# A fused attention and MLP kernel, re-planned: a longer transfer list for GpSimd, turned tiles stored by one transfer, a shorter weight decode, and three more chunks with halved own-key scores

## The chip, the cores and the metric

The kernel runs on one core of a Trainium2 chip. The metric is the device time of one execution in microseconds (us), less being better. The engines are called PE (TensorE, the matrix engine), DVE (VectorE), ACT (ScalarE), POOL (GpSimd) and SP (SyncE, which here only starts transfers). TensorE's weight loads (PEld) are listed apart from its matmuls (PE).

## The reference

Two sequences of S = 3136 tokens pass through three stages: an attention without softmax, a gated MLP with a convolution of three taps along the tokens, and a normalised MLP with a residual.

```python
scores = matmul(z, z.transpose(0, 2, 1)) / S          # z: 2 x 3136 x 64
x   = u * matmul(maximum(scores, 0) ** 2, v)          # u, v: 2 x 3136 x 256
h   = maximum(x @ w_in, 0)                            # 256 -> 1024
c   = conv of h over tokens, 3 taps per feature (conv_w), zero padded
x   = (h / (1 + exp(-c))) @ w_out                     # 1024 -> 256
xn  = (x - mean) / sqrt(var + 1e-6) * g_ln            # over the 256 features
out = x + maximum(xn @ w_ch1, 0) @ w_ch2
```

The weights arrive as float64.

## The kernel before

**Stages.** The 3136 queries of each sequence are cut into seven chunks of 4, 4, 3, 4, 3, 3 and 3.5 tiles of 128 (`TILES`), so there are 14 chunks, c = 0 to 13. For a chunk, each of the 25 key tiles j gives a score tile (two matmuls, `products`), which ACT passes through ReLU and squares, and which is split into a high part `ah` (a rounding cast) and a low part `al` (a subtraction on DVE), because each product is made of three matmuls, high by high, low by high and high by low (`av`). When all 25 keys are summed in the PSUM tile `av`, DVE multiplies by u (`gate_u`, op `gate_x`) and the result goes to DRAM. The MLPs run over 17 blocks of 384 or 256 tokens (`make_x`, `mlps`), interleaved with later chunks; the last two blocks, 256 tokens each, are the tail and share PSUM tiles.

**Scores used twice.** Scores are symmetric. A score tile of chunk c whose keys lie in a later chunk of the same sequence is turned 32 by 32 by DVE (`spill`, tile `bl`), stored to DRAM (`turned`), and loaded instead of computed when that later chunk comes (`land`, four transfers per tile, one for each group of 32 partitions, each by SP or POOL as the planner chooses). For four pairs of chunks (`EARLY`) the blocks are instead exchanged at the store: four transfers write `mirror`, and one transfer loads a tile. For the chunks in `HALVED`, the scores of a chunk's queries with its own keys are computed on one side of the diagonal alone (`corner` columns less); the other side is turned and stored (`spill_corner`) and loaded by four transfers per tile (`land_corner`).

**Weights.** Each of the 16 pieces of 512 weights per partition (and the small `conv_w`) is turned from float64 words into a high and a low float part by `decode`: ACT takes the absolute value, DVE makes several passes with integer operations, ACT or POOL casts and converts.

**Order.** A planner in the kernel's Python (`Program`) fixes the order of all instructions on each engine before anything runs. Every operation has a price (`PRICE`), a time after which others see its result (`AFTER`, `late`), and a due time that is worked back from its users; `once` plays the program through with these prices, always taking the ready operation that is due first, and `order` keeps the best of ten rounds. A block of the MLPs gets its due time from the end of its chunk plus a lag (`LAG0`, falling with c). POOL and SP take their instructions strictly in that order, transfers included. Where the plan leaves TensorE a gap, `fill` puts matmuls on a tile of zeros into it, one for each 0.125 us of planned gap (`FILL`), and twenty of them (`WARM`) stand ahead of everything.

[...]

## Time and profile before

| what | us |
|---|---|
| median of three runs | 1085.47 |
| lowest and highest | 1083.96 and 1085.91 |
| profiled execution, its own time | 1084.57 |
| span in the profile, first to last instruction | 1082.6 |

The profile gives busy time by engine, the span cut into 40 slices, the chain of work that ended last, groups of instructions by line, and who waited for whom. [...]

### The profile page before, as it was taken

The page shows a single profiled execution, that of the slowest core. Times are in us where ns is not written, and L with a number is a line of the kernel's source. Part 1 is how long each engine was busy: PE and PEld are TensorE (multiplying, and loading weights), DVE is VectorE, ACT ScalarE, POOL GpSimd, SP SyncE. Part 2 cuts the span into 40 slices and gives each one's busy share as a digit, 9 for nine tenths or more (in the row PEclk, how much of TensorE's full clock was granted, in tenths as well). Part 3 has the DMA queues.
Part 4 walks back from the last instruction along what each step waited for, and adds up shares of the span by engine and source line. Part 5 has one row for each costly group of instructions (what it writes and reads, how often), then busy time and mean ns, then how long its engine had stood idle before and what let it go on. Part 6 is the DMA issues. An engine that isn't in the chain of part 4 may idle for free.

```text
span 1082.6 us, 19738 instructions
## 1 busy us (share of the span) xinstructions
PE 1069.0 (99%) x6508; PEld 1008.7 (93%) x6508; DVE 873.6 (81%) x1888; ACT 732.6 (68%) x1530; POOL 170.7 (16%) x266
## 2 busy tenths in 40 slices
PE   9999999999999999999999999999999999999998
PEld 7777997999999999999999999999999999999998
DVE  7999998999887877787868879678778594878674
ACT  7788987777677766676757667566566474656553
POOL 2011112323131000000010101111222324310000
PEclk9999999999999999999999999999999999999999
DMA  6787867677677331324253424342644646430000
GB/s 205 203 210 159 211 164 172 163 179 194 177 177 180 97 112 49 102 80 124 55 134 103 120 52 122 93 110 66 151 89 109 139 94 153 97 85 26 18 23 21
DMA packets 312166, 130.42 MB, mean 120 GB/s; under 512 B 203920, under 2 KB 298528, under 8 KB 312064
## 3 DMA queue, kind: packets, MB, share of 16 engines
q1 hardware_dynamic: 304928, 117.49, 43.2%
q0 software_dynamic: 7136, 11.67, 4.9%
q8 instruction: 51, 0.84, 0.3%
q14 instruction: 51, 0.42, 0.1%
HBM read 72.21 MB, written 53.94 MB: 117 GB/s over the span
## 4 chain that ended last, share of the span: by engine, by line
PE 90%; DVE 3%; DMA 2%; issue 2%; ACT 2%; POOL 0%; SPq 0%; DVEq 0%; ACTq 0%
PE av L908 12%; PE av L911 12%; PE av L910 11%; PE y L1015 8%; PE y L1017 8%; PE y L1016 8%; PE h2ps L999 4%; PE hps L999 4%; PE h2ps L1000 4%; PE h2ps L1001 4%; PE hps L1001 4%; PE hps L1000 4%; PE s L866 3%; PE s L867 3%; DMA land<-turned 1%
## 5 line engine op out<-in xcount | busy, mean ns | idle before, releaser
L908 PE MATMUL av<-ah,vh 128*128 128x512 f32 (+2 forms) x700 | 257.0, 367 | 2.5 <-DVE u L926 2.1
L911 PE MATMUL av<-ah,vl 128*128 128x512 f32 (+2 forms) x700 | 256.0, 366 | 0.0
L910 PE MATMUL av<-al,vh 128*128 128x384 f32 (+2 forms) x672 | 246.7, 367 | 3.9 <-DVE al L842 3.9
L804 POOL DMA_DIRECT2D land<-turned x202 | 129.7, 643 | 449.4 <-DVE al L842 171.4
L908 PEld LDWEIGHTS av<-ah,vh 128*128 128x128 f32 x700 | 131.6, 188 | 14.6 <-DVE u L926 2.3
L911 PEld LDWEIGHTS av<-ah,vl 128*128 128x128 f32 x700 | 131.5, 188 | 14.3
L910 PEld LDWEIGHTS av<-al,vh 128*128 128x128 f32 x672 | 126.3, 188 | 16.1 <-DVE al L842 6.2
L1259 ACT ACTIVATE g2h<-h2ps 128x384 fp32r<-128x384 f32 (+1 forms) x136 | 65.2, 480 | 111.4 <-PE h2ps L1001 111.2
L1264 DVE SCALAR_TENSOR_TENSOR g2l<-h2ps,g2h 128x384 fp32r<-128x384 f32 (+1 forms) x136 | 72.8, 538 | 82.8 <-ACT g2h L1259 82.2
L875 ACT ACTIVATE a<-s 128x512 f32<-128x512 f32 (+3 forms) x196 | 102.0, 542 | 47.5 <-PE s L867 46.3
L842 DVE TENSOR_TENSOR al<-a,ah 128x512 fp32r<-128x512 f32 (+2 forms) x182 | 114.5, 639 | 4.4 <-ACT ah L459 3.5
L1015 PE MATMUL y<-w2h,g2h 128*128 128x256 f32 x392 | 110.2, 281 | 0.6 <-DVE ysb L1274 0.6
L1017 PE MATMUL y<-w2h,g2l 128*128 128x256 f32 x392 | 110.3, 281 | 0.0
L1016 PE MATMUL y<-w2l,g2h 128*128 128x256 f32 x392 | 110.0, 281 | 0.0
L1016 PE MATMUL y<-wol,gh 128*128 128x256 f32 x392 | 109.9, 280 | 0.0
L1015 PE MATMUL y<-woh,gh 128*128 128x256 f32 x392 | 109.9, 280 | 0.0
L1017 PE MATMUL y<-woh,gl 128*128 128x256 f32 x392 | 109.9, 280 | 0.0
L459 ACT CAST ah<-a 128x512 fp32r<-128x512 f32 (+2 forms) x187 | 106.8, 584 | 2.9 <-DVE a L880 0.7
L884 ACT ACTIVATE a<-a 128x512 f32<-128x512 f32 (+4 forms) x187 | 104.6, 577 | 1.7
L720 DVE STREAM_TRANSPOSE bl<-a 128x512 f32<-128x512 f32 (+1 forms) x146 | 94.3, 655 | 12.8 <-ACT a L884 12.1
L1035 ACT ACTIVATE h<-hps 128x386 f32<-128x386 f32 (+1 forms) x136 | 64.8, 480 | 52.6 <-PE hps L1001 51.5
L1050 DVE SCALAR_TENSOR_TENSOR t<-h,cw,t 128x384 f32<-128x384 f32 (+1 forms) x136 | 80.6, 597 | 22.8 <-ACT t L1041 22.3
(119 smaller groups left out, 2545.4 us busy)
## 6 DMA issues: line engine op xcount, KB each, us to landing
turned<-bl SPq DMA_DIRECT2D x78, 256.0 KB, 2.4
land<-turned SPq DMA_DIRECT2D x189, 48.0 KB, 2.6
turned<-bl SPq DMA_DIRECT2D x44, 192.0 KB, 2.7
out_dram<-ysb SPq DMA_DIRECT2D x15, 384.0 KB, 2.7
vst<-in_v_dram SPq DMA_DIRECT2D x11, 512.0 KB, 4.7
xl<-gated SPq DMA_DIRECT2D x14, 386.0 KB, 4.0
centred<-tn SPq DMA_DIRECT2D x14, 384.0 KB, 2.8
tn<-centred SPq DMA_DIRECT2D x56, 96.0 KB, 2.6
```

The costliest lines, as they stand in the source:

```text
L459: nc.scalar.copy(dst, src)
L720: [("DVE", price("dve_turn", w))], lambda e: nc.vector.transpose(at(b, "bl")[:, :w], at(ab)[:, :w]),
L804: ISSUE[e].dma_start(out=at(b, "land")[o * SQ : (o + 1) * SQ, :n].rearrange("p (g k) -> p g k", k=SQ), in_=blocks_[o, :, g0 : g0 + n // SQ ...
L842: lambda e: nc.vector.tensor_tensor(at(al, "al")[:, :n], a(), f(at(ah)[:, :n]), ALU.subtract),
L875: [("ACT", price("act_ps", n))], lambda e: nc.scalar.activation(a(), at(ps)[:, :n], AF.Relu),
L884: op([("ACT", price("act", n))], lambda e: nc.scalar.activation(a(), a(), AF.Square), writes=[(ab, "own")], name="square")
L908: nc.tensor.matmul(p, vhj, at(ah)[:, :n], start=first(b, d), stop=False, **kw)
L910: nc.tensor.matmul(p, vhj, at(al)[:, :n], start=False, stop=False, **kw)
L911: nc.tensor.matmul(p, vlj, at(ah)[:, :n], start=False, stop=False, **kw)
L1015: nc.tensor.matmul(p, a, wh, start=first(acc, (i0 + i) // 2), stop=False, **kw)
L1016: nc.tensor.matmul(p, a, wl, start=False, stop=False, **kw)
L1017: nc.tensor.matmul(p, b, wh, start=False, stop=k == NF - 1, **kw)
```

## The change

- `HALVED` gains the chunks c = 4, 5 and 6.
- `EARLY` is empty: all turned tiles are stored by one transfer and loaded by four.
- The list space is 2048 bytes (`RING` = 128 entries), and the planner now holds a POOL transfer back until its entries (`descs`, 33 for a 512-wide tile, 25 for 384) are free.
- `decode` makes three DVE passes instead of four for the high part: a scale of 2^-112 in ACT's absolute value makes the lower clamp and one of the shifts unnecessary.
- `LAG0` is 100 instead of 130, and the planner sees the result of `gate_x` 0.3 us later than before (`TURNS`).
- The last block sums its second MLP in a PSUM tile of its own (`av`) instead of the half of the tile `y` that it shared with the block before.
- Three small tiles for `conv_w` go, its words use places of `h`; the tile of zeros is 128 wide instead of 256, and a filler is now two matmuls of 128 columns instead of one of 256.

```diff
-LAG0 = 130.0
+LAG0 = 100.0
-HALVED = 7, 8, 9, 10, 11, 12, 13
-EARLY = (0, 5), (0, 6), (1, 5), (1, 6)
+HALVED = 4, 5, 6, 7, 8, 9, 10, 11, 12, 13
+EARLY = ()
-RATE, LANDS = 300.0, 1.6
+RATE, LANDS, BACKS = 300.0, 1.6, 0.5
-LANES = 8
+LANES, RING = 8, 128
+TURNS = {"gate_x": 0.3, "ysb": 0.0, "residual": 0.0}
...
                     for _ in range(o.dmas):
-                        t = max(t, lanes[e].pop(0)) + us / o.dmas
+                        t = max(t, lanes[e].pop(0))
+                        if e == "POOL":
+                            while sum(n for at, n in ring if at > t + 1e-9) + o.descs > RING:
+                                t = min(at for at, _ in ring if at > t + 1e-9)
+                            ring = [(at, n) for at, n in ring if at > t + 1e-9]
+                        t += us / o.dmas
...
+                        if e == "POOL":
+                            ring.append((moved_at + LANDS + BACKS, o.descs))
...
-        op([("ACT", price("act_scale", n_))], lambda e: nc.scalar.activation(f(c()), f(hi()), AF.Abs), reads=[sk], writes=[(cb, 0)], name="abs")
+        op([("ACT", price("act_scale", n_))], lambda e: nc.scalar.activation(f(c()), f(hi()), AF.Abs, scale=2.0**-112), reads=[sk], writes=[(cb, 0)], name="abs")
         steps = [
-            (d1, lambda e: vec.tensor_scalar(f(c()), f(c()), MIN_HI, MAX_HI, ALU.max, ALU.min), (cb, 0), ()),
-            (d1, lambda e: vec.tensor_scalar(c(), c(), 4, 0x80000000, ALU.logical_shift_left, ALU.bitwise_xor), (cb, 0), ()),
-            (d1, lambda e: vec.tensor_scalar(c(), c(), 1, 0x7FFFF000, ALU.logical_shift_right, ALU.bitwise_and), (cb, 0), ()),
+            (d1, lambda e: vec.tensor_scalar(f(c()), f(c()), MAX_HI, None, ALU.min), (cb, 0), ()),
+            (d1, lambda e: vec.tensor_scalar(c(), c(), 3, 0x7FFFF000, ALU.logical_shift_left, ALU.bitwise_and), (cb, 0), ()),
...
-                reads=[(b, d)], writes=[(u, d)], name="gate_x",
+                reads=[(b, d)], writes=[(u, d)], late=AFTER["DVE"] + TURNS["gate_x"], name="gate_x",
...
-        acc2 = shared("y") if tail else buf("y", True)
+        acc2 = shared("y") if c == NK - 2 else buf("av" if c == NK - 1 else "y", True)
...
-    zero = const.tile([P, 256], F32R, name="zero")
+    zero = const.tile([P, P], F32R, name="zero")
...
-        for _ in range(n):
-            nc.tensor.matmul(to, zero[:, :P], zero, start=start, stop=start, skip_group_check=True)
+        for _ in range(2 * n):
+            nc.tensor.matmul(to[:, :P], zero, zero, start=start, stop=start, skip_group_check=True)
...
-    nc = _bacc.Bacc("TRN2", target_bir_lowering=False, num_devices=1, dynamic_dma_scratch_size=1024)
+    nc = _bacc.Bacc("TRN2", target_bir_lowering=False, num_devices=1, dynamic_dma_scratch_size=RING * 16)
```

## Rows read from the trace of the kernel before

**Rows 1.** The page: busy us, share, instructions; then a window, PE, PEld, DVE, ACT, POOL.

```profile
PE 1069.0 (99%) x6508; PEld 1008.7 (93%) x6508; DVE 873.6 (81%) x1888; ACT 732.6 (68%) x1530; POOL 170.7 (16%) x266
...
27.00:300.00 273.00, 267.91 (x1426) 242.60 (x1425) 252.08 (x514) 216.33 (x445) 55.01 (x83) 1.00 0.76 184
```

**Rows 2.** What TensorE waited for: total us, times, longest.

```profile
PE av L910 <- DVE al L842: 3.9, 4, 2.5
PE av L908 <- DVE u L926: 2.1, 6, 0.4
PE s L866 <- ACT a L875: 1.2, 1, 1.2
...
PE y L1015 <- DVE ysb L1274: 0.6, 1, 0.6
```

**Rows 3.** Timeline 160 to 180: start us, duration, engine, line, operation [idle before <-releaser].

```profile
166.26 0.65 POOL L804 DMA_DIRECT2D land<-turned  x1 [2.77 <-DVE wc L583]
...
167.27 1.30 DVE L720 STREAM_TRANSPOSE bl<-a 128x512 f32<-128x512 f32 x2 [0.64 <-ACT a L884]
...
170.52 0.66 POOL L804 DMA_DIRECT2D land<-turned  x1 [3.61 <-issue]
...
171.86 0.43 DVE L590 TENSOR_SCALAR wc<-wc 128x512 uint32<-128x512 uint32 x1 [3.28 <-POOL w1h L461]
...
172.94 0.50 PE L910 MATMUL av<-al,vh 128*128 128x512 f32 x1 [2.46 <-DVE al L842]
...
173.28 0.40 PE L911 MATMUL av<-ah,vl 128*128 128x512 f32 x1
```

**Rows 4.** Timeline of POOL, 54 to 70; and its waits over the span.

```profile
62.96 0.65 POOL L804 DMA_DIRECT2D land<-turned  x1 [2.61 <-issue]
...
POOL land L804 <- issue: 74.5, 49, 4.1
```

**Rows 5.** Timeline of TensorE at the end: the chain, then the start, 0 to 30.

```profile
1070.01 0.38 PE y L1015
...
1.20 4.26 PE L1388 MATMUL warm_ps<-zero 128*128 128x256 f32 x20 [1.20 <-DVE zero L1383]
5.82 0.50 PE L866 MATMUL s<-hl 128*128 128x512 f32 x1 [0.37 <-DVE hl L500]
...
8.03 1.59 PE L1388 MATMUL warm_ps<-zero 128*128 128x256 f32 x12
9.45 0.39 PE L908 MATMUL av<-ah,vh 128*128 128x512 f32 x1
10.74 0.50 PE L910 MATMUL av<-al,vh 128*128 128x512 f32 x1 [0.90 <-DVE al L842]
```

**Rows 6.** Timeline of weight loads: two beside matmuls of 128 columns, then beside 512.

```profile
761.30 0.19 PEld L867 LDWEIGHTS s<-lh,hl 128*128 128x128 f32 x1
761.41 0.19 PEld L866 LDWEIGHTS s<-hl 128*128 128x128 f32 x1
761.52 0.19 PEld L867 LDWEIGHTS s<-lh,hl 128*128 128x128 f32 x1
761.75 0.19 PEld L1015 LDWEIGHTS y<-woh,gh 128*128 128x128 f32 x1
```

**Rows 7.** By line: the removed DVE pass, the mirrored stores (ns min/median/max).

```profile
L582 DVE TENSOR_SCALAR wc<-wc x17: 170/416/428, 47.3 to 275.2; 128x512 uint32<-128x512 uint32 x16, 128x24 uint32<-128x24 uint32 x1
...
L735 SPq DMA_DIRECT2D mirror<-bl x52: 302/504/1194, 48.4 to 108.9; - x52
```

**Rows 8.** Window 234 to 290, clock and DMA share near its end; transfers; queue, 48 to 62.

```profile
234.00:290.00 56.00, 56.00 (x345) 55.76 (x344) 50.15 (x110) 40.55 (x87) 13.21 (x19) 1.00 0.68 174
...
DMA packets 18538, 9.77 MB, mean 174 GB/s; under 512 B 12501, under 2 KB 17493, under 8 KB 18533
...
land<-mirror SPq DMA_DIRECT2D x8, 192.0 KB, 2.9
...
q1 hardware_dynamic: 9488, 1.95, 71.8%
```

## The prediction

> **What bounds the kernel now.** I read the page first, then TensorE's waits, then the timeline around each of them. TensorE is busy 1069.0 of 1082.6 us, DVE 873.6 [rows 1]. That leaves 13.6 us without a matmul, and only there, in the fillers, or in matmuls that are no longer made can time be won. TensorE's waits [rows 2] show what the idle time is: 3.9 us in four waits for a low part `al`, 2.1 us in six waits for `gate_x` at the turn from one chunk to the next, 1.2 us once for ACT, 0.6 us near the end. Most of the rest is the start and the last transfer, and the change leaves the last transfer alone. So the prize is 3.9 + 2.1 + 1.2 + 0.6 = 7.8 us, 0.7% of the time, and what the new plan gets wrong is paid out of the same purse. From 27 to 300 us DVE is busy 252.08 of 273 us, 92%, against 81% over the span [rows 1]; there the decode of the weights runs, and there three of the four waits for `al` lie.

> **Scores (removal on the path).** A chunk with three whole own tiles now computes 384, 256 and 128 columns instead of three times 384, twice each; c = 6 computes 448, 320 and 192. Columns saved: 2 x 384 in each of three chunks, 2304. Weight loads beside matmuls of 512 columns follow each other after 0.23 us, 0.45 ns a column [rows 6], so 1.04 us. But a short matmul isn't paid by its columns: beside those of 128 the loads follow after 0.11 us, not 0.058 [rows 6]. That takes 0.05 us from each of the two matmuls of the shortest tile in c = 4 and 5, less in c = 6, together some 0.2: **0.9 us** gained (0.8 to 1.0). TensorE is full there, so it reaches the end. Added: six transposes, 256 and 128 wide, each under the 0.65 us of a 512-wide one (1.30 for two [rows 3]), so under 3.9 us of DVE, six stores and 24 small loads; ACT gets less ReLU and square to do. Their cover is DVE's idle time, 5.9 us in 234 to 290 alone [rows 8]; without it up to 3.9 us.

> **POOL's list (the largest term).** The longest wait of TensorE, 2.46 us at 172.94, can be followed back step by step [rows 3]: TensorE waits for `al`; DVE stood 3.28 us ahead of its pass at 171.86, waiting for POOL's cast `w1h`; that cast was queued on POOL behind the load at 170.52; and that load was held 3.61 us by nothing the profile can name. I read it as the list: a 512-wide load takes 33 of 64 entries, so a second does not fit until the first has landed. The spacing bears it out: 166.26 to 170.52 is 4.26 us, and at the load at 62.96 stands the same unnamed wait, 2.61 us; 49 such waits make 74.5 us of POOL [rows 4]. With 128 entries three fit, the cast runs about 3.6 us earlier, DVE is not stopped, and its `al` is ready before TensorE asks. Gain 2.46, and 0.1 more because the first matmul after a wait is followed after 0.34 us [rows 3] instead of 0.23: **2.6 us**. Late next would be DVE, which would then run without a gap. Since the planner now also counts entries, it will not queue a cast behind a load that can't start.

> [...]

> **Turn of chunks.** Six waits for `gate_x`, 2.1 us [rows 2], lie where TensorE needs the PSUM tile that DVE still reads. The plan believed the result to be there 0.3 us earlier than it is. Told so, it can put 0.3 us of MLP matmuls in front. Where none is ready the wait stays. Between 0 and 2.7 us (2.1 and six restarts at 0.1); I take half, **1.3 us**.

> **Tail.** TensorE waited 0.6 us for the residual of the last but one block, then its first matmul stood 0.38 us in the chain [rows 2, 5], where 256 columns at 0.45 ns make 0.12. With its own PSUM tile the last block does not wait: 0.8 us, of which I take **0.7**.

> **Decode.** 16 passes at 0.416 and a short one of 0.17 us leave DVE: 6.8 us [rows 7], all before 275 us. It's time on the path only where TensorE waits for DVE: of the 3.9 us of `al` waits, 0.9 is the start [rows 5], 2.5 is counted above, and 0.5 is left. Gain 0 to 0.5, taken **0.4**.

> **Stores of turned tiles.** 14 tiles leave by 14 instead of 56 transfers (52 are on record), 42 x 0.504 = 21.2 us of SP's queue gone between 48 and 109 us [rows 7], and SP's loads for chunk 1 no longer queue behind them. No wait of TensorE there is SP's alone, so 0 (up to 0.3 gain). In exchange 16 tiles are loaded by 64 instead of 16 transfers, in 234 to 290 us: see the rivals.

> **Fillers (a loss).** One filler of 256 columns becomes two of 128, each with its own weight load. The planner still reckons 0.125 us. At 0.11 us a load [rows 6] the pair takes 0.22. The 12 fillers at 8.03 lasted 1.4 us up to their successor at 9.45 [rows 5]; 24 short ones take 2.6, 1.2 us more, against a wait of 0.9 us that stands behind them. [...] Part of both is swallowed by the waits for the first v and z, so together **+1.5** at the start (0 to +3.0), and **+0.3** for fillers later on.

> [...]

> **The sum.** -0.9 - 2.6 - 1.3 - 0.7 - 0.4 + 1.5 + 0.3 = -4.1 us. The profiled execution took 1084.57 (span 1082.6 and 2.0 around it), the median of the runs is 1085.47. From the profiled one 1080.5, from the median 1081.4: **1081.0**. Its own range: with every gain in full and no filler cost -1.0 - 2.6 - 2.7 - 0.8 - 0.5 - 0.3 = -7.9, about 1077; with fillers at +3.3 and no gain at the turns 1085.5 - 0.9 - 2.6 - 0.7 + 3.3 = 1084.6.

> **Rivals.**

> [...]

> *The new plan trades waits.* `LAG0` falls by 30, so the MLPs of the early chunks become due sooner and pull their DVE work into a stretch where DVE is already at nine tenths [rows 1]. Every step has a price in the plan, but the 7 us of idle middle show how much such prices miss, and a new order misses elsewhere. If new waits as large as all those for `al` (3.9 us [rows 2]) come on top of the sum, it is 1081 + 3.9 = 1084.9: no change.

> *Slower: the loads of chunks 5 and 6 come late.* Place: 234 to 290 us. The share of the DMA engines there is 0.68, 38 of 56 us [rows 8]. Price of a small packet: in 48 to 62, mostly mirrored stores, 9488 packets took 71.8% of 14 us, 1.06 ns each [rows 8]. 16 tiles in pieces of 128 bytes are 8 x 128 x 12 + 8 x 128 x 14 = 26,624 packets, 28 us; the row-wise loads they replace go, 8 of 192 KB and 8 of 224, 3.4 of the 9.77 MB moved there [rows 8], so a third of the 38 us, 13 us. So 53 of 56 us. It decides from the point where the engines are full; then each of some four loads that is not fetched ahead costs about 2 us of waiting: 1081 + 8 = 1089. Against it: some loads go by POOL, the planner charges loads for nearly twice their bytes, and `a` has places to fetch ahead.

> **How the numbers follow.** Forecast 0.56 (1081.0), list not the cause 0.14 (1083.6), waits traded 0.16 (1084.9), late loads 0.14 (1089). About 0.2%, 2.2 us, is what a measurement of this kernel can tell from no change, so the bounds are 1083.3 and 1087.7. Of the forecast's own range nearly all lies below 1083.3; of the second case half. Faster 0.61, same 0.22, slower 0.17. The range is 1075.5 to 1088.0: the forecast's low end with some of the 1.2 us wait for ACT gone too, and the nearer part of the late loads.

> **What would show it.** Right: no TensorE wait over 1 us in 100 to 300; POOL's 512-wide loads starting within 0.7 us of each other; the sum of POOL's unnamed waits well under 74.5; no wait of y for the residual near 1070; fewer than six waits for `gate_x`. For the fillers: the first score tile later than 5.82, fillers starting 0.11 us apart or more. Wrong: new waits for `al` whose chain ends in a landing between 230 and 300 with a DMA share near 1, or a cast on POOL still held behind a load.

## The result and the profile after

| | before | after |
|---|---|---|
| median of six runs each, us | 1085.15 | 1092.93 |
| lowest and highest, us | 1083.76 and 1086.06 | 1091.13 and 1097.45 |
| profiled execution, us | 1084.57 | 1091.13 |
| span of its profile, us | 1082.6 | 1089.4 |

The ratio is 1.0077, 95% interval 1.0057 to 1.0097: the change makes the kernel **slower by 7.8 us** (8.4 by the ratio), where 4.1 us faster was predicted. The profiled execution of before had a granted clock of 1.00; of the 71 executions of before that were run beside the experiments 36 had 0.999 or 1.000 and took 1083.9 us in the mean, 35 had 0.998 or less and took 1086.5.

The page of the changed kernel, engines (busy us, share, instructions), and three stretches of its windows (length, then PE, PEld, DVE, ACT, POOL busy, granted clock, DMA share, GB/s):

```profile
PE 1083.0 (99%) x6588; PEld 1025.0 (94%) x6588; DVE 876.9 (80%) x1887; ACT 725.8 (67%) x1519; POOL 188.4 (17%) x299
...
8.00:12.00 4.00, 4.00 (x15) 3.52 (x15) 0.52 (x1) 0.89 (x2) 0.49 (x1) 1.00 0.45 147
...
27.00:300.00 273.00, 272.52 (x1488) 248.69 (x1488) 255.17 (x515) 216.14 (x447) 61.72 (x97) 1.00 0.74 175
234.00:290.00 56.00, 56.00 (x363) 55.86 (x362) 50.93 (x116) 38.51 (x83) 16.34 (x27) 1.00 0.68 140
```

What the changed kernel's engines waited for (total us, times, longest), POOL's unnamed wait and all of TensorE's:

```profile
POOL land L815 <- issue: 14.2, 13, 3.1
...
PE warm_ps L1399 <- DVE zero L1394: 1.1, 1, 1.1
PE av L919 <- DVE u L937: 0.7, 2, 0.4
PE av L921 <- DVE al L853: 0.5, 2, 0.3
```

Against [rows 1, 2] the puzzle is plain: most of the waits that were to go are gone (of 7.8 us 1.2 are left), TensorE stands 6.4 us instead of 13.6, and the kernel is slower. Its busy time has grown by 14 us. No new wait stands behind the first fillers; the time is inside the matmuls. The start of TensorE's timeline shows the first part (start us, duration, line, operation):

```profile
1.06 8.79 PE L1399 MATMUL warm_ps<-zero 128*128 128x128 f32 x40 [1.06 <-DVE zero L1394]
9.65 0.73 PE L877 MATMUL s<-hl 128*128 128x512 f32 x1
10.19 0.63 PE L878 MATMUL s<-lh,hl 128*128 128x512 f32 x1
10.61 0.63 PE L877 MATMUL s<-hl 128*128 128x512 f32 x1
11.04 0.63 PE L878 MATMUL s<-lh,hl 128*128 128x512 f32 x1
...
12.32 0.58 PE L1399 MATMUL warm_ps<-zero 128*128 128x128 f32 x4
12.74 0.45 PE L877 MATMUL s<-hl 128*128 128x512 f32 x1
13.03 0.39 PE L878 MATMUL s<-lh,hl 128*128 128x512 f32 x1
13.26 2.79 PE L1399 MATMUL warm_ps<-zero 128*128 128x128 f32 x24
15.89 0.45 PE L919 MATMUL av<-ah,vh 128*128 128x512 f32 x1
16.17 0.39 PE L921 MATMUL av<-al,vh 128*128 128x512 f32 x1
```

The same place before, between the lines of [rows 5]:

```profile
6.16 0.40 PE L867 MATMUL s<-lh,hl 128*128 128x512 f32 x1
6.39 0.39 PE L866 MATMUL s<-hl 128*128 128x512 f32 x1
...
7.32 0.40 PE L1388 MATMUL warm_ps<-zero 128*128 128x256 f32 x2
```

The forty short fillers take 8.6 us, 0.215 each, so the first score tile starts at 9.65, not 5.82 [rows 5]: 3.8 us late. The score matmuls behind them, from the second on, start 0.42 to 0.43 us apart until about 12.3; before, they started 0.23 apart. (The granted clock reads 1.00 in this stretch all the same, as the window from 8 to 12 us shows. The trace's record of the clock begins only at 12.36 us here and at 4.86 before, and there the pace changes: here from 0.43 us per 512 columns to 0.23, before from 0.213 us a filler up to 4.78 to 0.12 from 4.94 on. So at the start, here and in [rows 5], the level is read from the pace. The record has two values in both traces, 1.00 and 0.50; the changed kernel has 0.50 from 1087.6 us on, behind its last matmul. "Lower level" means that value below, and at the start the slower pace.) The later 24 fillers take 2.63 us, 0.110 each, where 12 wide ones took 1.42. In exchange the wait for `al` behind them is gone. The first `av` on `al` starts at 16.17 instead of 10.74: **5.4 us lost before anything else has happened.**

The rest is spread out. The mean step from one matmul to the next of the same shape and tile, worked out from the start times after 20 us (longer steps, with a wait in them, left out), in ns, for all kernels that matter below:

```
kernel                        y 256   av 384   av 512
before                        117.9    174.4    233.0
e4_list_before                117.9    174.4    232.9
e3_short_before               117.9    174.4    233.0
after                         119.4    176.0    232.1
e1_wide                       119.4    176.0    232.2
e8_wide_nofill                119.4    176.0    232.1
e7_wide_list64                119.4    176.0    232.1
e5_wide_shift32               117.4    174.4    233.8
e9_short_shift32              117.4    174.4    233.8
e10_wide_shift64              117.1    174.8    233.2
e13_wide_shift64_again        117.1    175.0    233.3
e14_undo_all_but_list         117.0    175.1    233.2
e6_before_shift32             116.7    174.0    229.4
e11_list_before_shift32       116.6    173.9    229.4
```

Between before and after, the 2352 matmuls of y lose 1.5 ns each, 3.5 us, and some 750 steps each of `av` lose 1.6 and win 0.9 ns. That makes about 4 us that no wait shows, at the same granted clock.

### The profile page after: what moved, and what is told of

The parts are those of the page before. It is cut to its first block, busy times and chain, and to the rows that moved or that the text cites. A ratio compares the mean times of both kernels' runs of the same rounds, so it can differ in the third digit from the quotient of the medians.

```text
span 1089.4 us, 20001 instructions
## 1 busy us (share of the span) xinstructions
PE 1083.0 (99%) x6588; PEld 1025.0 (94%) x6588; DVE 876.9 (80%) x1887; ACT 725.8 (67%) x1519; POOL 188.4 (17%) x299
## 4 chain that ended last, share of the span: by engine, by line
PE 97%; DVE 1%; ACT 1%; DMA 1%; issue 0%; SPq 0%; DVEq 0%; ACTq 0%
PE av L919 13%; PE av L922 13%; PE av L921 12%; PE y L1028 9%; PE y L1026 9%; PE y L1027 8%; PE hps L1012 4%; PE hps L1011 4%; PE hps L1010 4%; PE h2ps L1010 4%; PE h2ps L1011 4%; PE h2ps L1012 4%; PE s L878 3%; PE s L877 3%; PE warm_ps L1399 2%; DMA land<-turned 1%
## 5 line engine op out<-in xcount | busy, mean ns | idle before, releaser
L815 POOL DMA_DIRECT2D land<-turned x227 | 144.1, 638 | 336.8 <-DVE al L853 193.4
L886 ACT ACTIVATE a<-s 128x512 f32<-128x512 f32 (+4 forms) x196 | 102.5, 536 | 52.8 <-PE s L878 52.3
L731 DVE STREAM_TRANSPOSE bl<-a 128x512 f32<-128x512 f32 (+1 forms) x146 | 95.0, 657 | 13.2 <-ACT a L895 12.4
L895 ACT ACTIVATE a<-a 128x512 f32<-128x512 f32 (+5 forms) x187 | 104.0, 570 | 1.7
L853 DVE TENSOR_TENSOR al<-land,ah 128x384 fp32r<-128x384 f32 (+2 forms) x154 | 90.2, 594 | 8.3 <-ACT ah L463 7.0
```

Source lines behind the costliest of these rows:

```text
L731: [("DVE", price("dve_turn", w))], lambda e: nc.vector.transpose(at(b, "bl")[:, :w], at(ab)[:, :w]),
L815: ISSUE[e].dma_start(out=at(b, "land")[o * SQ : (o + 1) * SQ, :n].rearrange("p (g k) -> p g k", k=SQ), in_=blocks_[o, :, g0 : g0 + n // SQ ...
L853: lambda e: nc.vector.tensor_tensor(at(al, "al")[:, :n], a(), f(at(ah)[:, :n]), ALU.subtract),
L886: [("ACT", price("act_ps", n))], lambda e: nc.scalar.activation(a(), at(ps)[:, :n], AF.Relu),
L895: op([("ACT", price("act", n))], lambda e: nc.scalar.activation(a(), a(), AF.Square), writes=[(ab, "own")], name="square")
```

## The experiments

Theory after the comparison: the short fillers cost what the change brings and more. First rival: the new order is worse by itself. Second: something slows the matmuls all along the span. "Wide" is one filler matmul of 256 columns as before (the 128-wide tile of zeros is read twice), "short" is two of 128.

**e1_wide: the change with wide fillers.** All else, the order and the places of all tiles included, stays.

```diff
-        for _ in range(2 * n):
-            nc.tensor.matmul(to[:, :P], zero, zero, start=start, ...)
+        for _ in range(n):
+            nc.tensor.matmul(to.rearrange("p (a b) -> p a b", a=2), zero, zero.unsqueeze(1).to_broadcast([P, 2, P]), ...)
```

> The changed kernel with one edit: a filler is again one matmul of 256 columns (the same 128 columns of zeros read twice), so the 20 at the start and those in the gaps have half the weight loads. Theory (the fillers' shape made the loss): in the changed kernel the first av matmul by al starts at 16.17 us against 10.74 before, and 86 short fillers in the gaps run at about 0.11 us each, 43 pairs at 0.22 where the plan reckons 0.125. With wide fillers the start returns to about 10.8 (-5.4 us) and the gaps shrink by up to 43 x 0.1 = 4.3 us, of which I expect half because waits return: 1092.9 - 5.4 - 2.2 = about 1085, between 1082 and 1087. Rival (the new order of work, or late landings of chunks five and six, made the loss): the time stays at 1090 or above although the fillers are back.

Measured: 1084.7 us, ratio to before 0.9992 [0.9982, 1.0001]. The start is that of before again:

```profile
1.06 4.31 PE L1399 MATMUL warm_ps<-zero 128*128 128x256 f32 x20 [1.06 <-DVE zero L1394]
5.83 0.50 PE L877 MATMUL s<-hl 128*128 128x512 f32 x1 [0.47 <-DVE hl L504]
...
8.01 1.59 PE L1399 MATMUL warm_ps<-zero 128*128 128x256 f32 x12
...
10.65 0.50 PE L921 MATMUL av<-al,vh 128*128 128x512 f32 x1 [0.81 <-DVE al L853]
```

So the short fillers cost 8.2 us by the medians, 9.2 by the ratios. But with wide ones the change brings nothing, where it should then bring some 5.

**e2_warmwide: only the twenty fillers ahead of everything wide,** those in gaps short (`fill(WARM, ...)` is replaced by twenty wide matmuls).

> The changed kernel with only the 20 matmuls ahead of everything wide again; the fillers in the gaps stay two of 128 columns. It parts the start from the rest. [...] Rival (the start does not reach the end, because data arrive late anyway): 1092 or more.

Measured: 1086.67 us, 1.0019 [1.001, 1.0029], where about 1088.5 was expected. The first score tile starts at 5.54 us, and from its third matmul on they are 0.23 us apart. By the ratios the twenty are 6.3 us of the loss and the fillers in gaps, those at the start behind the twenty included, 2.9.

**e3_short_before: the kernel before, only its fillers short.**

```diff
-    zero = const.tile([P, 256], F32R, name="zero")
+    zero = const.tile([P, P], F32R, name="zero")
...
-        for _ in range(n):
-            nc.tensor.matmul(to, zero[:, :P], zero, ...)
+        for _ in range(2 * n):
+            nc.tensor.matmul(to[:, :P], zero, zero, ...)
```

> The kernel before with that one part of the change alone: every filler two matmuls of 128 columns, the order of all else untouched. Theory: the start costs 5.4 us as in the changed kernel, and 14 later pairs (26 less the 12 at 8.03) 0.1 us each at most: 1085.2 + 5.4 + 1.0 = about 1091.5. If fillers cost nothing here, the loss belongs to the rest of the change: 1085 to 1086.

Measured: 1092.8 us, 1.0074 [1.0056, 1.0093]. This one edit alone makes the kernel before as slow as the whole change does, so the fillers are shown from both sides. That the two losses are equal is in part luck, for here some of it goes another way, as a wait over the span and a window show:

```profile
PE av L910 <- DVE al L842: 4.3, 4, 3.1
...
180.00:200.00 20.00, 20.00 (x89) 16.75 (x90) 18.32 (x36) 14.14 (x29) 6.14 (x9) 0.93 0.69 161
```

The start is as slow as in the change (in the first 27 us TensorE is busy 25.94 us in both, DVE 16.33 and 16.26 against 21.17 in before). But the wait of [rows 3] grows from 2.46 to 3.1 us, and the granted clock from 180 to 200 us is 0.93, the lower level for an estimated 3 us (0.07 of 20 us, at half the clock): together some 2 us that belong to the list.

**e4_list_before: the kernel before with the longer list alone** (1728 bytes instead of 1024; at the 16 bytes an entry that the change counts, `RING * 16`, 108 entries instead of 64), order untouched, wide fillers (a 128-wide tile of zeros, read twice, makes room for it).

```diff
-    nc = _bacc.Bacc("TRN2", ..., dynamic_dma_scratch_size=1024)
+    nc = _bacc.Bacc("TRN2", ..., dynamic_dma_scratch_size=1728)
```

> The kernel before with its list space alone enlarged, from 64 to 108 entries (three loads of 33 fit), and wide fillers read from 128 columns of zeros twice to make room; the order is untouched. Theory of the prediction (the list held POOL): the wait of 2.46 us at 172.9 goes, POOL's unnamed waits of 74.5 us fall under 15 us, and the time falls by 2.6 us or a little more: about 1082.5. Rival (something else held POOL): waits and time as before, 1085.

Measured: 1081.5 us, 0.9967 [0.9955, 0.9979], 3.6 us faster. Its waits:

```profile
POOL land L804 <- issue: 13.2, 16, 4.0
...
PE av L908 <- DVE u L926: 2.1, 6, 0.4
PE s L866 <- ACT a L875: 1.2, 1, 1.2
PE av L910 <- DVE al L842: 1.1, 2, 0.6
```

POOL's unnamed waits fall from 74.5 us to 13.2, and the 2.46 us wait for `al` is gone [rows 2, 4], though no instruction has changed its place in the order. So it was the space of the list that held POOL. All six executions have a granted clock of 0.999 or 1.000. Now the change as a whole, with wide fillers, is slower than this part of it.

**e7_wide_list64: e1 with the short list,** 1024 bytes again under an order that was planned for 128 entries.

```diff
-    nc = _bacc.Bacc("TRN2", ..., dynamic_dma_scratch_size=RING * 16)
+    nc = _bacc.Bacc("TRN2", ..., dynamic_dma_scratch_size=1024)
```

> The changed kernel with wide fillers (as e1), its order untouched, but the list space of before, 64 entries. Theory (the list is the gain that e4 showed): POOL's unnamed waits rise from 8.6 us to 75 us or more, and since this order queues more loads on POOL (227 against 202) TensorE waits 3 to 8 us more: 1088 to 1093. Rival (the order, which counts entries, had made the space unnecessary): 1085.

Measured: 1101.68 us, 1.0148 [1.0105, 1.0191], 17 us slower than e1. POOL's unnamed waits are back and TensorE pays for them, most between 200 and 300 us, as the waits over the span, then the window and two matmuls in it show:

```profile
POOL land L815 <- issue: 85.8, 58, 4.2
...
PE av L919 <- ACT ah L463: 4.3, 4, 2.2
PE av L921 <- DVE al L853: 2.9, 5, 2.0
```

```profile
200.00:300.00 100.00, 94.01 (x558) 90.18 (x557) 81.23 (x186) 62.08 (x139) 33.51 (x52) 0.97 0.65 139
...
214.07 0.44 PE L919 MATMUL av<-ah,vh 128*128 128x384 f32 x1 [2.17 <-ACT ah L463]
215.15 0.52 PE L919 MATMUL av<-ah,vh 128*128 128x384 f32 x1
```

e1, with the long list, has 99.69 us of matmuls in the same stretch, at 1.00. Behind waits of 2.17 and 1.41 us TensorE ran at the lower level here for part of the time (granted clock 0.97 from 200 to 300 us): 384 columns took 0.32 us from 215.15 to 218.03 and again from 225.41 to 227.33, instead of 0.18 ahead of the first wait.

**e8_wide_nofill: e1 without fillers planned after 20 us** (35 wide ones left of 63).

> The changed kernel with wide fillers, but none in gaps that the plan has after 20 us; the order of all else is untouched. e1 made 28 such fillers, about 3.3 us of TensorE. Theory (they delay work that would be ready): 1084.7 - 1 to 3 = 1082 to 1084, with waits on DVE in their place for the rest. Rival (the gaps are real, and the fillers only stand where TensorE would be idle): 1084.7, with 3 us of idle time in their place; if the clock falls for lack of work, slower.

Measured: 1083.78 us, 0.9985 [0.9967, 1.0002]; 0.7 us by the ratio, too little to tell from none. Without them the granted clock is 0.999 or 1.000 in all ten executions.

**e5_wide_shift32: e1 with 32 unused bytes per partition** between the constant tiles (weights, zeros) and the working tiles. In the change, three small tiles are gone and two sizes have changed, so all working tiles lie elsewhere. This moves them on by 32 bytes and adds nothing but one memset of the padding on POOL.

```diff
     zero = const.tile([P, P], F32R, name="zero")
+    pad = const.tile([P, 8], F32, name="pad")
+    nc.gpsimd.memset(pad, 0.0)
```

> The changed kernel with wide fillers (as e1) and 32 bytes of padding ahead of the working tiles, so that `ah`, `al`, `xh` begin on a multiple of 64 bytes again, as in the kernel before, while `gh`, `gl`, `xth` lose that. In e1 TensorE stood idle 5.3 us less than in the kernel before and yet took as long, because matmuls of the same shape followed each other more slowly (256 columns of y after 119.4 ns against 117.9, 384 columns of av after 176 to 177 against 175). Theory (the place of the tiles in SBUF, changed because three small tiles are gone, sets that pace): av of 384 columns returns to 175 ns and the time falls by 1.5 to 4 us, to 1081 to 1083. Rival (the pace comes from the order of the instructions): pace and time stay, 1084.7.

Measured: 1080.17 us, 0.9959 [0.994, 0.9977]. Same instructions in the same order, but for that memset, and 4.5 us faster (3.6 by the ratios). The groups of y on TensorE (count, then busy us and mean ns of one), in e1:

```profile
L1026 PE MATMUL y<-w2h,g2h 128*128 128x256 f32 x392 | 110.8, 283 | 0.0
...
L1027 PE MATMUL y<-wol,gh 128*128 128x256 f32 x392 | 110.4, 282 | 0.0
```

and in e5:

```profile
L1026 PE MATMUL y<-w2h,g2h 128*128 128x256 f32 x392 | 109.9, 280 | 0.0
...
L1027 PE MATMUL y<-wol,gh 128*128 128x256 f32 x392 | 109.6, 279 | 0.0
```

The step of y falls from 119.4 to 117.4 ns: 2352 x 2.0 = 4.7 us, the whole gain. The steps of `av`, for which it was expected, fall by 1.6 and rise by 1.7 ns and cancel.

**e6_before_shift32: the same 32 bytes in the kernel before.**

> The kernel before with 32 bytes of padding ahead of the working tiles and nothing else; the order is untouched, all working tiles lose their place on multiples of 64 bytes. Theory (place sets the pace): y of 256 columns slows from 117.9 to about 119.5 ns, av of 384 from 175 to 176.5, and the time rises by 3 to 5 us, to 1088 to 1090. Rival (the order sets it): no change, 1085.

Measured: 1.0012 [0.9993, 1.0031], no gain, though every step in the table is shorter than in before, where longer ones were expected. Where the gain went is seen in POOL's timeline,

```profile
173.46 0.66 POOL L804 DMA_DIRECT2D land<-turned  x1 [4.57 <-issue]
174.14 0.63 POOL L461 TENSOR_SCALAR w1h<-wc 128x512 fp32r<-128x512 f32 x1
```

in TensorE's,

```profile
175.88 0.80 PE L910 MATMUL av<-al,vh 128*128 128x512 f32 x1 [5.21 <-DVE al L842]
176.48 0.63 PE L911 MATMUL av<-ah,vl 128*128 128x512 f32 x1
176.90 0.63 PE L908 MATMUL av<-ah,vh 128*128 128x512 f32 x1
177.33 0.63 PE L910 MATMUL av<-al,vh 128*128 128x512 f32 x1
```

and in the window (columns as above):

```profile
160.00:180.00 20.00, 14.79 (x67) 12.34 (x66) 13.53 (x27) 11.12 (x21) 4.08 (x6) 0.83 0.77 168
```

It is the wait of [rows 3], now 5.21 us instead of 2.46. POOL's load stands 4.57 us for nothing that the profile names, the cast `w1h` stands behind it, DVE behind the cast. After 5.21 us without a matmul TensorE runs at 0.43 us per 512 columns for 3.6 us, and the granted clock of the stretch is 0.83, the lower level for part of it. All ten executions of e6 have a granted clock of 0.997 or less.

**e11_list_before_shift32: e4 and e6 together,** the kernel before with the longer list and the 32 bytes.

> The kernel before with the long transfer list (1081.5 us) and 32 unused bytes ahead of its working tiles. In the kernel before with the short list the 32 bytes quickened the pace of y from 118.2 to 117.0 ns but the time did not fall, with one wait of 5.2 us for al and a dip of the granted clock between 100 and 200 us. Theory A (that dip hangs on GpSimd's late loads): with the long list it is gone and the quicker pace pays, about 1081.5 - 3 = 1078.5 us at a clock of 0.999 or more. Theory B (the quicker pace is what draws the throttle): clock about 0.996 again and 1081 to 1084 us.

Measured: 1077.11 us, 0.9924 [0.9908, 0.994], **the lowest median of the study**. With the list long enough the wait is gone and the shorter steps pay. Its window from 100 to 200 us shows TensorE busy throughout at a clock of 1.00:

```profile
100.00:200.00 100.00, 100.00 (x542) 91.37 (x541) 95.99 (x197) 88.08 (x187) 21.10 (x33) 1.00 0.81 180
```

**e9_short_shift32: the change as it is, short fillers, with the 32 bytes.**

> The change exactly as it is, its narrow fillers included, with 32 unused bytes ahead of the working tiles. Theory A (fillers and placement are two separate losses that add up): the fillers' 8.2 us stay and the placement's 4.5 us go, so about 1092.9 - 4.5 = 1088.4 us and a mean step of y's 256-column matmuls of about 117.8 ns instead of 119.8. Rival B (the 32 bytes gained only in company with the wide fillers): about 1092.9 us.

Measured: 1089.28 us, 1.0028 [1.0011, 1.0045]. Fillers and places add up: 3.6 us less than the change by the medians, 9.1 more than e5.

**e10_wide_shift64: e1 with 64 unused bytes instead of 32.**

> The change with wide fillers and 64 unused bytes ahead of the working tiles instead of 32. Theory A (only where a tile starts within 64 bytes counts): the tiles start where they did without any padding, within 64 bytes, so the pace of y falls back to about 119.5 ns and the time to about 1084.7 us. Theory B (the address counts in some other way, or any padding does): a pace other than 119.5 ns and a time away from 1084.7 us, near 1080 to 1082 us.

Measured: 1078.31 us, 0.9939 [0.9921, 0.9957]. My theory A, that only the start within 64 bytes counts, falls: the tiles start within 64 bytes where they did in e1, and the step of y is 117.1 ns, not 119.4. That the place counts stands: the kernels with the same places have the same steps in the table to 0.3 ns, on more than one chip, whatever else differs (after, e1, e8; e5, e9; e10, e13, e14).

The addresses narrow it further. `gh` and `gl`, which y loads as weights, lie at the same bytes in e4 and e14 (outside the tail), and y takes 117.9 and 117.0 ns; so their own address does not set the pace. And where everything moved so that the distance from the constant tiles (the streamed weights) to the working tiles stayed or changed by 512 bytes, the steps stayed: in e4 the first moved by 704 and the second by 192 bytes, in e3 by 0 and -512, in e7 against e1 both by -1024. Padding changes that distance by 32 or 64. That the distance is what counts fits all these kernels; no run was made to test it.

**e12_wide_shift32_nofill: e5 without the fillers after 20 us.**

> The change with wide fillers, 32 unused bytes, and no fillers in the gaps after the start (37 wide ones fewer). Theory A (each gap filler costs what it runs, as the pair without padding showed with 1084.7 to 1083.8 us): about 1080.2 - 0.9 = 1079.3 us. Rival B (without them TensorE idles where it ran them, and nothing is won): 1080.2 us.

Measured: 1080.0 us, 0.9951 [0.9934, 0.9968], against 0.9959: 0.9 us by the ratios, within the intervals, of the same sign as in e8 (28 fillers fewer here too, not 37). Left open.

**The rest of the change, at fixed places** (all but five tiles, the largest `xth` and `xtl`, lie where they did in e10). Four kernels on one chip: e10 once more (e13); e13 with all of the change undone but list and places (e14); with scores and decode undone (e15); with the 0.3 us after `gate_x` and the tail's own tile undone (e16).

```diff
# e14: e15, e16 and
-LAG0 = 100.0
+LAG0 = 130.0
-EARLY = ()
+EARLY = (0, 5), (0, 6), (1, 5), (1, 6)
# e15
-HALVED = 4, 5, 6, 7, 8, 9, 10, 11, 12, 13
+HALVED = 7, 8, 9, 10, 11, 12, 13
...
# e16
-TURNS = {"gate_x": 0.3, "ysb": 0.0, "residual": 0.0}
+TURNS = {"gate_x": 0.0, "ysb": 0.0, "residual": 0.0}
-        acc2 = shared("y") if c == NK - 2 else buf("av" if c == NK - 1 else "y", True)
+        acc2 = shared("y") if tail else buf("y", True)
```

> The change with wide fillers and 64 unused bytes once more, as the base of the next three on the same chip: 1078.3 us as measured.

Measured: 1077.9 us, 0.9942 [0.9929, 0.9954].

> The same with all of the change undone but the long list and the tiles' places: scores whole in chunks five and six of the first two rounds, decode with its third pass, no time reserved after the gates, one PSUM bank shared in the tail, the old lag and early list of the order. Theory A (the four small terms came as predicted): 1078.3 + 0.9 + 1.3 + 0.7 + 0.4 = 1081.6 us. Theory B (the new order gives back what they bring, as the planner's own totals say, 1067.1 before and 1069.0 after): 1078 us or less.

Measured: 1080.36 us, 0.9961 [0.9949, 0.9974]. The rest of the change is worth 2.5 us by the medians, 2.1 by the ratios.

> The base with only the scores whole in chunks four, five and six and the decode's third pass back. Theory A: the prediction's terms, 1078.3 + 0.9 + 0.4 = 1079.6 us. Theory B (scores that are not halved leave the order less broken up, so nothing is lost): 1078.3 us or less.

Measured: 1078.93 us, 0.995 [0.9936, 0.9963]: 0.9 us by the ratios.

> The base with only the time reserved after the gates gone and the tail's bank shared again. Theory A: the gate waits and the tail wait come back, 1078.3 + 1.3 + 0.7 = 1080.3 us, and VectorE's u and al stand among the waits of TensorE with more than 2 us. Theory B (the long list already took the waits away): 1078.3 us with the waits as in the base.

Measured: 1083.34 us, 0.999 [0.9978, 1.0001], 5.2 us slower by the ratios, where 2.0 was expected. The profiled execution, 1085.4 us, is one of the slower of the eleven. The tail's wait is back as it stood before:

```profile
1069.59 0.28 PE L1028 MATMUL y<-w2h,g2l 128*128 128x256 f32 x1
1070.44 0.39 PE L1026 MATMUL y<-w2h,g2h 128*128 128x256 f32 x1 [0.58 <-DVE ysb L1285]
```

From 1069.59 to 1070.44 is 0.85 us where a step is 0.12: 0.73 us. The gates' waits are not back (1.1 us in three). What fills the rest are waits in other places, such as

```profile
352.78 0.39 PE L1026 MATMUL y<-woh,gh 128*128 128x256 f32 x1 [1.20 <-DVE gh L467]
```

A changed price makes another order, and other orders miss by some microseconds, here or there. e14, which undoes these two parts as well, waits 1.2 us or more only once, 1.3 us for ACT, which before did too. So what e15 and e16 give is as much the accidents of an order as the worth of a part.

## Why the prediction was wrong

By the ratios (times 1085 us), a walk from before to after in kernels that were run:

| step | from, to | us | predicted |
|---|---|---|---|
| longer list | before, e4 | -3.6 | -2.6 |
| places, that of e13 against that of before | e4, e14 | -0.6 | none |
| scores, turns, tail, decode, order | e14, e13 | -2.1 | -3.3 |
| places, that of the change against that of e13 | e13, e1 | +5.4 | none |
| short fillers | e1, after | +9.2 | +1.8 |
| sum | | +8.4 | -4.1 |

From e4 to e14 TensorE's order differs in 30 of 6508 positions; besides the places, the list grows from 108 to 128 entries, the words of `conv_w` lie in `h`, and the other engines' orders shift a little. Each single step is uncertain by 1.3 to 2.4 us, so the -0.6 can't be told from none. The miss of 12.5 us is 7.4 from the fillers and 4.8 from the places; the two other terms miss by about a microsecond each, in opposite directions.

**Fillers: the step that failed.** The prediction named the right place, two matmuls and two weight loads in place of one, and priced the 24 behind the first score tiles well, at 2.6 us where 2.63 were measured. But its +1.5 for the start was the author's estimate, and no run shows it; the runs showed 5.4, beyond the +3.0 at which its range was cut. The first forty took 0.215 us each, twice the 0.11 of [rows 6], and the first score tile started at 9.65. The pace did not rise while they ran, only under the score tiles behind them: 0.43 us per 512 columns up to 12.32 us (record of the clock from 12.36), against 0.23 us from 6.16, 6.17, 6.53 and 6.61 us on in the timelines of before, e1, e2 and e4, all with twenty wide ones. Why the shape matters, no run shows. So the six score matmuls were paid at the lower pace too (2.67 us for 1.50), which the sum did not have at all. By pieces: 3.83 late, 1.17 there, 0.23 up to the next fillers, 1.21 for the 24, less 1.01 for the wait that it swallowed, 5.4 together. So +1.5 at the start measured 5.4. The "+0.3 for fillers later on" was too small as well: the kernel before has 12 fillers behind the first 16 us, the change 29 pairs, and at 0.1 us more for a pair that is an estimated 2.9 us. The planner went on pricing a pair at 0.125 us and so filled gaps of the plan with twice as much as they hold.

**Places: the step that was missing.** The prediction treats the tiles that go and the sizes that change as free. They move every working tile, and the steps of TensorE follow the place. This could not be read from the trace of before. From e13 to e1 the steps give 2352 x 2.3 for y, and for some 750 steps each 1.0 and -1.1 for `av`: 5.3 us, where the times give 5.4. Why a place is good or bad stays open; not the clock, not the fillers, not TensorE's order, not the start within 64 bytes, and not the address of the tiles loaded as weights (`gh`, `gl`) by itself. The weights that stream through in y did not move in e5 and e10; the working tiles all moved together, and no run tells apart which of them, or which distance, counts.

**The list: right,** and undersized by 1.0 us, which is within the error and has a source on record. The prediction read one execution at full clock; beside e4, before has nine such executions (0.999 or 1.000) at 1084.5 us in the mean and twelve with 0.998 or less at 1086.1. Against the first e4 gains 3.0 us, against the second 4.6. That the second kind fell to the lower level behind the wait that the list made, as the traces of e3 and e6 with the same list show it, is argued: no trace of such an execution was kept, but none of the 15 executions of e4, e11 and e14, with the longer list, is below 0.999. e4 shows the chain gone, e6 the same chain at a quicker pace, and e7 that an order planned for the long list needs it. The longer list took 61 of POOL's 74.5 us of unnamed waits away. That a 512-wide load takes 33 entries is the change's own count (`descs`); the runs show only what the space does.

**Turns, tail, scores, decode: right in kind,** 2.1 to 2.5 us of the 3.3. Waits for `gate_x` went from six, 2.1 us, to two, 0.7; predicted was 1.3 of gain. The tail's 0.7 measured 0.73. Scores and decode measured 0.9 for 1.3, within the error.

**The rivals.** That the list is not the cause, given 0.14 with 1083.6 us, is refuted by e4: 1081.5 us and 13.2 us of unnamed waits with the space and the tile of zeros alone changed. "The new plan trades waits" did not happen: 1.2 us of waits behind the first matmul are left. "The loads of chunks 5 and 6 come late" did not happen: from 234 to 290 TensorE is busy 56.00 of 56 us, and the DMA share is 0.68, as in [rows 8], not near 1. The forecast of a DMA share of 53 in 56 us was wrong too: the loads by pieces did not fill the engines as reckoned. Slower came by none of them: the one term that the sum counted as a loss was put too low, and the places were not in it.

## What to carry to other kernels

Price a filler, and those at the start above all, by the pace measured where it runs, and look at the pace of the matmuls behind it: here twenty matmuls of 256 columns took 4.3 us and the score matmuls were 0.23 us apart from 6.2 to 6.6 us on, and forty of 128 took 8.6 us and the score matmuls behind them stayed at 0.43 up to 12.3. A change that frees or resizes a tile can move other tiles, as here it moved all working tiles; before judging such a change (or a few tenths of a per cent of any), run it with a few bytes of padding, for here 32 or 64 bytes (e1 to e5 and e10, 3.6 and 5.8 us by the ratios) were worth as much as the best idea in it (the list, 3.6). The kernel before with a longer list, a narrower tile of zeros and 32 bytes of padding, three small edits, is at 1077.1 us level with the whole change at its best place tried (1077.9; the intervals overlap) and well ahead of what it came from (1085.2). And look at the clock of every execution of the base, not only of the profiled one: half of them had a loss that the profile did not show.
